# Loading x tile 0 through two queues, a later logarithm of the variances, and a new order of the leading TensorE work

## The chip, the cores and the metric

One Trainium2 chip, of which the kernel uses 1 core. The metric is the device time of one execution in microseconds (us), lower is better. The core has five engines that run at once: TensorE (PE, matrix multiply; its weight loads are shown apart as PEld), VectorE (DVE), ScalarE (ACT), GpSimd (POOL) and SyncE (SP, which here only issues transfers). ACT and POOL can issue transfers too. An engine takes its own instructions in order and waits for other engines on semaphores.

## The reference

Two branches over the same 2048 tokens of width 512 are mixed by a gate per token. Branch A is attention in a window of 8 keys at distance 2, with 32 heads of width 16. Branch B is a layer norm, followed by an MLP over the token axis.

```python
qkv = (x @ wqkv).reshape(B, S, 3, H, Dh)            # S 2048, D 512, H 32, Dh 16
idx = pos[:, None] - off[None, :]                   # off = 0, 2, ..., 14
logits = einsum("bhsd,bhswd->bhsw", q, kg) * scale  # masked where idx < 0
o = einsum("bhsw,bhswd->bhsd", softmax(logits), vg)
a = o.reshape(B, S, D) @ wo

h = (x2 - mean(x2)) / sqrt(var(x2) + 1e-5)          # over D, per token
u = gelu(einsum("bsd,sf->bdf", h, w1) + b1)         # S 2048, F 1792
y = einsum("bdf,fs->bds", u, w2) + b2
b = y.transpose(0, 2, 1)

g = sigmoid((x * gate_w).sum(-1, keepdims=True))
out = g * a + (1 - g) * b
```

The kernel takes the same x for both branches, and all tensors are bf16.

## The kernel before

Tokens come in 16 tiles of 128 rows. The work on TensorE has a fixed order, since each piece that is added through the helper `PE` (L570) is ordered behind the piece before it. On the other engines a list scheduler (`_Sched`, L75) sets the order from assumed durations and priorities, and the waits follow from which resource each operation reads and writes (`add`, L92). An `after` argument orders an operation behind the start of another one, without a semaphore.

TensorE goes through these stages.

- The head: six matmuls of ones (`f_warm`, L564), transposes of the tiles 0 to 3 of x (`tx`, L579), transposes of the biases b1 and b2 (`f_tb`, L594 and L595), a broadcast of the gate vector (L634), and the "leads" (L651 and L610). A lead t multiplies a strip of w1 (`lw`) with the normalized tile t (`lx`) into the banks 0 to 3. Lead 0 is done in two column halves.
- The projections of q, k and v (L716), whose input is x transposed. Their banks are 4 to 7, in a ring.
- The first MLP matmul (`f_ph2`, L601), with two sums of logits between (`f_sum`, L807).
- The second MLP matmul (`f_ph3`, L941) with the output projection (`f_wo`, L950), tile by tile, and the stores.

In the head, each of the first four tiles goes through a chain on two engines. On DVE there are `stat` (L615) and `aggr` (L619), which give mean and variance. On ACT, `rstd` (L622 and L623, both recorded under L469) takes a logarithm and an exponential, which need the table that ACT loads first (L1032). Then DVE normalizes the tile (`apply` L626, or L643 for the two halves of tile 0), and the lead may start. ACT copies transposed tiles out of PSUM (`ext`, L591), and the gate broadcast out of bank 6 (`evgw`, L659). Bank 6 also receives the transposes of tile 2, and bank 7 both those of tile 3 and the biases.

The tiles 4 to 15 are normalized later, all at once: DVE takes the statistics (L779) and combines them (L782 to L788), ACT takes the logarithm (`ln_log`, L789) and the exponential (`ln_rstd`, L790), DVE makes `ln_nmr` (L791). The tiles are then normalized in place by ACT (L795) for the last `LNACT` = 11 tiles, each ordered behind one copy of a projection out of PSUM (`ev2`, L748), and by DVE (L798) for the others, here tile 4 only. DVE also makes 16 gate sums (`z`, L760), which read the tiles of x before they are normalized, and the whole of the attention (L466).

Loads are issued on the queue of SP in the order of the program (`load`, L491, whose `order` argument chains them). Three small ones are on ACT's queue: b1, b2 and the gate vector. The very first load on SP's queue is tile 0 of x:

```python
def ld_x(t0, n):
    load("x%d" % t0, X[:, t0:t0 + n, :], xv[:, t0:t0 + n, :], n * 128 * D * 2, ["x%d" % t for t in range(t0, t0 + n)])

ld_x(0, 1)
ld_x(1, 1)
```

Of the kernel before, what the change touches and what calls it, by code (L numbers as in the profile page):

```python
# [9 lines left out]
AF = mybir.ActivationFunctionType  # L10
# [3 lines left out]
D = 512  # L14
# [14 lines left out]
NLEAD = 4  # L29
AVD = (1, 3, 5, 6)  # L30
GL = 4
NOUT = 8
LNACT = 11


class _Op:
# [281 lines left out]
def bass_gated_mix__sliding_local_dilated__mixer_token_mlp__prompt_kernel(nc, A_x, A_wqkv, A_wo, B_x, B_w1, B_b1, B_w2, B_b2, gate_w, out, dbg=None):  # L318
    with contextlib.ExitStack() as es:
# [39 lines left out]
        A = sch.add  # L359

        x2d = A_x[0]
# [6 lines left out]
        X = view("X", BF16, [(D, NST), (1, D)])  # L368
# [7 lines left out]
        def w2view(name, extra=0):  # L376
            return view(name, BF16, [(256, NFT), (1, 256)], extra=extra)

        XTALL = ["xt0_%d" % t for t in range(4)] + ["xt1", "xt2", "xt3"]
        W2S = [w2view(*W1SLOT[2]), w2view(*W1SLOT[3]), w2view(*W1SLOT[4]), w2view("P2"), w2view(*W1SLOT[0]), w2view(*W1SLOT[1]),  # L380
               w2view("X"), w2view("X", NFT * 256)]
        W2ALIAS = [["w1s2"], ["w1s3"], ["w1s4"], ["p2"], ["w1s0"], ["w1s1"],
                   ["x%d" % t for t in range(7)], ["x%d" % t for t in range(7, 14)]]
        XTUSE = ["w1s3", "w1s4"]
        PR = [["p0", "p0b"], ["p1", "p1b"], ["p2", "p2h"], ["log0", "log1", "att0", "att1", "lw0", "lw1", "lw2", "lw3", "gwr"]]
        LW = view("LOG", BF16, [(128 * GL, NLEAD), (1, 128 * GL)])
# [42 lines left out]
        ST6 = small(6 * NST, [(6, NST), (1, 6)])  # L429
# [8 lines left out]
        VV = small(NST)  # L438
# [6 lines left out]
        Z = small(NST)  # L445
# [6 lines left out]
        def col(v_, i):  # L452
            return bass.AP(v_.tensor, v_.offset + i, [list(v_.ap[0]), [1, 1]])
# [7 lines left out]
        def psub(ap_, p0, np_, offs, dims):  # L461
            pst = ap_.ap[0][0]
            return bass.AP(ap_.tensor, ap_.offset + p0 * pst + offs, [[pst, np_]] + [list(d) for d in dims])
# [4 lines left out]
        def act(o_, i_, f_, **kw):  # L468
            return lambda e: e.activation(out=o_, in_=i_, func=f_, **kw)  # L469
# [21 lines left out]
        def load(name, dst, src, nbytes, writes, transpose=False, queue="sp", issue=0.5, order=True, deps=(), reads=()):  # L491
            ds = sch.dsem(name)

            def fn(e):
                if transpose:
                    return e.dma_start_transpose(dst, src)
                return e.dma_start(dst, src)
            op = sch.dma(queue, fn, nbytes, ds, issue=issue, reads=reads, writes=writes, deps=deps,
                         after=([last_ld[0]] if order and last_ld[0] is not None else []), name=name)
            if order:  # L500
                last_ld[0] = op
            return op

        def ld_x(t0, n):
            load("x%d" % t0, X[:, t0:t0 + n, :], xv[:, t0:t0 + n, :], n * 128 * D * 2, ["x%d" % t for t in range(t0, t0 + n)])
# [11 lines left out]
        def ld_strip(t, n):  # L517
            load("s%d" % t, LW[:, t:t + n, :], w1v[:, t:t + n, 0:128 * GL], n * 32768 * GL, ["lw%d" % t_ for t_ in range(t, t + n)])

        ld_x(0, 1)  # L520
        ld_x(1, 1)
        ld_strip(0, 1)
        ld_x(2, 1)
# [46 lines left out]
        def PE(fn, dur, reads, writes, name, prio=0):  # L570
            op = A("pe", fn, dur, reads=reads, writes=writes, after=([chain[0]] if chain[0] is not None else []), name=name, prio=prio)
            chain[0] = op
            return op

        def f_tx(t):
            def fn(e):
                ins = None
                for dt in range(4):
                    ins = e.transpose(out=psb(4 + t)[:, dt * 128:dt * 128 + 128], in_=X[:, t, dt * 128:(dt + 1) * 128], identity=IDENT)  # L579
                return ins  # L580
            return fn

        def tx(t):
            PE(f_tx(t), 0.4, ["x%d" % t, "ident"], ["b%d" % (4 + t)], "tx%d" % t)

        def ext(t, eng, after):
            src = sub(psb(4 + t), 0, [(128, 4), (1, 128)])
# [24 lines left out]
            return fn  # L612

        def stat(t, after):
            return A("dve", (lambda t_: lambda e: e.bn_stats(out=ST6[:, t_, :], in_=X[:, t_, :]))(t), (0.69 if t == 0 else 0.58), reads=["x%d" % t], writes=["st%d" % t],  # L615
              after=after, name="st%d" % t, prio=-40)

        def aggr(t, after=()):
            return A("dve", (lambda t_: lambda e: e.bn_aggr(out=AG[:, t_, :], in_=ST6[:, t_, :]))(t), 0.17, reads=["st%d" % t], writes=["ag%d" % t], after=after, name="ag%d" % t, prio=-40)  # L619
# [5 lines left out]
        def apply(t, after):  # L625
            return A("dve", (lambda t_: lambda e: e.tensor_scalar(out=LX[:, t_, :], in0=X[:, t_, :], scalar1=AG[:, t_, 0:1], scalar2=col(RSTD, t_),  # L626
                                                                  op0=ALU.subtract, op1=ALU.mult))(t), 0.41, reads=["rstd%d" % t, "st%d" % t, "x%d" % t],
                     writes=["lx%d" % t], after=after, name="ln%d" % t, prio=-40)
# [1 line left out]
        PE(f_warm(6, 0), 2.6, [], ["b0"], "warm0")  # L630
        tx(0)
        tx(1)
        PE(f_tb, 0.2, ["b1r", "b2r", "ident"], ["b7"], "t_b12")
        PE(lambda e: e.matmul(ps[:, 6, :], lhsT=psub(WONE, 0, 1, 0, [(0, 128)]), rhs=GW1, start=True, stop=True), 0.4, ["gwr"], ["b6"], "gwbc")  # L634
        def lead(t):
            PE(f_lead(t), 0.87, ["lx%d" % t, "lw%d" % t], ["b%d" % ft for ft in range(GL)], "lead%d" % t)
# [5 lines left out]
        for q_ in range(2):  # L642
            l0 = A("dve", (lambda c_: lambda e: e.tensor_scalar(out=LX[:, 0, c_:c_ + 256], in0=X[:, 0, c_:c_ + 256], scalar1=AG[:, 0, 0:1],  # L643
                                                                scalar2=col(RSTD, 0), op0=ALU.subtract, op1=ALU.mult))(256 * q_), 0.22,
                   reads=["rstd0", "x0"], writes=["lx0%s" % "ab"[q_]], name="ln0%s" % "ab"[q_], prio=-40)
        e0 = ext(0, "act", [r0])
        def f_lead0(c0):
            def fn(e):
# [9 lines left out]
        r1 = rstd(1)  # L658
        ew = A("act", act(GWB, ps[:, 6, :], AF.Copy), 0.6, reads=["b6"], writes=["gwb"], after=[r1], name="evgw", prio=-50)  # L659
        tx(3)  # L660
        tx(2)
        s2 = stat(2, [ag])
        l1 = apply(1, [s2])
        ag = aggr(2, [l1])
        r2 = rstd(2)
        s3 = stat(3, [ag])
# [4 lines left out]
        e2 = ext(2, "act", [e1])  # L671
        e3 = ext(3, "dve", [l2])
        l3 = apply(3, [e3])
        for t in range(1, NLEAD):
            lead(t)
        e3 = l3
        A("dve", lambda e: e.tensor_copy(out=B1C, in_=psb(7)[:, 512:512 + NFT]), 0.15, reads=["b7"], writes=["b1c"], after=[e3], name="b1c", prio=-20)
        A("dve", lambda e: e.tensor_copy(out=B2C, in_=psb(7)[:, 544:544 + NST]), 0.15, reads=["b7"], writes=["b2c"], after=[e3], name="b2c", prio=-20)
# [57 lines left out]
        for dl in range(4):  # L736
# [3 lines left out]
          reads=["k%d_1" % dl for dl in range(4)], writes=["khalo"], name="khalo")  # L740
# [10 lines left out]
        ev2 = [[]]  # L751
# [6 lines left out]

        for t in range(NST):
            A("dve", (lambda t_: lambda e: e.tensor_tensor_reduce(out=JUNK[:, t_ % 4, :], in0=X[:, t_, :], in1=GWB, scale=1.0, scalar=0.0, op0=ALU.mult, op1=ALU.add,  # L760
                                                                  accum_out=col(Z, t_)))(t), 0.61, reads=["x%d" % t, "gwb", "s4"], writes=["z%d" % t, "jk%d" % (t % 4)], after=[e3],
              name="z%d" % t, prio=-4)
        A("pool", lambda e: e.memset(ZN, 0.0), 0.15, writes=["zn"], name="zn0")
        A("dve", lambda e: e.tensor_scalar(out=ZN[:, 0:NST], in0=Z, scalar1=ZMAX, scalar2=-1.0, op0=ALU.min, op1=ALU.mult), 0.12,
          reads=["z%d" % t for t in range(NST)], writes=["zn"], name="zneg", prio=-30)
# [20 lines left out]
        A("dve", lambda e: e.tensor_scalar(out=MS, in0=MS, scalar1=0.5, scalar2=None, op0=ALU.mult), 0.12, writes=["ms"], name="ln_mean", prio=-20)  # L786
        A("dve", lambda e: e.scalar_tensor_tensor(out=VV, in0=MD, scalar=128.0, in1=VV, op0=ALU.mult, op1=ALU.add), 0.12,
          reads=["md"], writes=["vv"], name="ln_var", prio=-20)  # L788
        A("act", act(VV, VV, AF.Ln, bias=1e-5, scale=1.0 / 512), 0.25, writes=["vv"], name="ln_log", prio=-20)  # L789
        A("act", act(RSTD2, VV, AF.Exp, scale=-0.5), 0.25, reads=["vv"], writes=["rstd"], name="ln_rstd", prio=-20)  # L790
        A("dve", lambda e: e.scalar_tensor_tensor(out=NMR, in0=MS, scalar=-1.0, in1=RSTD2, op0=ALU.mult, op1=ALU.mult), 0.12,  # L791
          reads=["ms", "rstd"], writes=["nmr"], name="ln_nmr", prio=-20)
# [290 lines left out]
```

## Time and profile before

| | us |
|---|---|
| median of 3 runs | 163.98 |
| lowest and highest of them | 163.47, 164.33 |
| the profiled execution | 163.24 |
| its span in the profile | 162.0 |
| of the span: TensorE busy | 159.0 |
| VectorE busy | 150.3 |
| ScalarE busy | 79.2 |
| GpSimd busy | 26.7 |
| head of TensorE, until the first projection matmul starts | 8.97 |

The profile describes one execution, from its first recorded instruction to its last. That span is 1.2 us shorter than the time of the same execution, and the time of the same execution is 0.7 us below the median of the three runs. A busy TensorE isn't TensorE at its peak, since matmuls overlap and their ends are modelled. How far apart matmuls start says more: in the projections 192 of them take 41.44 us, 0.216 us each.

### The profile page before, as it was taken

How to read it: one execution, taken by the hardware profiler on the slowest of the kernel's cores; microseconds unless marked ns; L12 is line 12 of the kernel's file. 1: busy time of each engine (PE TensorE's matmuls, PEld its weight loads, DVE VectorE, ACT ScalarE, POOL GpSimd, SP SyncE). 2: the span in 40 equal slices, each digit the busy share in tenths (PEclk: the TensorE clock that was granted, in tenths of full speed). 3: DMA queues.
4: the chain of work that ended last, by engine and by line, in shares of the span. 5: the costliest groups of instructions: out<-in, count | busy, mean ns of one | idle time of the engine just before them, and what ended most of it. 6: DMA issues, size and time to landing. Idle time of an engine off the chain costs nothing.

```text
span 162.0 us, 2018 instructions
## 1 busy us (share of the span) xinstructions
PE 159.0 (98%) x783; PEld 76.5 (47%) x783; DVE 150.3 (93%) x142; ACT 79.2 (49%) x105; POOL 26.7 (17%) x62
## 2 busy tenths in 40 slices
PE   7999999999999999999999999999999999999994
PEld 3555555555554344444444344444444444444652
DVE  2969999999999999999899999999999999999933
ACT  3727765799999472999211346320111111111153
POOL 3000011000000020200891030008770003020000
DMA  4999999999923999998499999999999815949404
GB/s 136 273 230 273 192 302 279 256 213 213 329 58 85 302 290 257 235 271 161 123 319 366 328 295 262 248 312 290 318 199 223 181 43 112 184 111 195 117 32 162
DMA packets 45288, 35.54 MB, mean 219 GB/s; under 512 B 8030, under 2 KB 42079, under 8 KB 45279
## 3 DMA queue, kind: packets, MB, share of 16 engines
q1 hardware_dynamic: 41376, 22.74, 53.0%
q0 software_dynamic: 3696, 12.59, 36.0%
q8 instruction: 6, 0.10, 0.3%
q10 hardware_dynamic: 206, 0.08, 0.2%
q14 instruction: 4, 0.02, 0.0%
HBM read 19.15 MB, written 2.11 MB: 131 GB/s over the span
## 4 chain that ended last, share of the span: by engine, by line
PE 98%; DVE 0%; issue 0%
PE ps L941 30%; PE ps L601 28%; PE ps L716 26%; PE ps L950 9%; PE ps L564 2%; PE ps L610 2%; PE ps L807 1%; PE ps L579 1%; PE ps L651 1%; DVE arena L959 0%; PE ps L634 0%; PE ps L594 0%; PE ps L595 0%
## 5 line engine op out<-in xcount | busy, mean ns | idle before, releaser
L466 DVE TENSOR_TENSOR arena<-arena 128x4096 bf16<-128x4096 bf16 (+8 forms) x71 | 125.8, 1806 | 1.7 <-DMA arena<-arena 0.5
L941 PE MATMUL ps<-arena 128*128 128x512 bf16 (+2 forms) x238 | 50.2, 366 | 0.0
L469 ACT ACTIVATE arena<-ps,arena 128x512 bf16<-128x512 f32 (+1 forms) x29 | 20.9, 728 | 56.5 <-PE ps L950 40.0
L601 PE MATMUL ps<-arena 128*128 128x512 bf16 x208 | 45.4, 379 | 0.0
L716 PE MATMUL ps<-arena 128*128 128x512 bf16 x192 | 41.6, 379 | 0.0
L469 ACT ACTIVATE arena<-ps 128x512 bf16<-128x512 f32 (+3 forms) x38 | 31.6, 843 | 11.0 <-PE ps L716 8.5
L941 PEld LDWEIGHTS ps<-arena 128*128 128x128 bf16 x238 | 23.3, 98 | 25.4
L601 PEld LDWEIGHTS ps<-arena 128*128 128x128 bf16 x208 | 20.2, 98 | 24.9 <-issue 0.8
L716 PEld LDWEIGHTS ps<-arena 128*128 128x128 bf16 x192 | 21.7, 113 | 19.8 <-ACT arena L469 0.2
L469 ACT ACTIVATE arena<-arena 128x512 bf16<-128x512 bf16 (+6 forms) x29 | 16.9, 581 | 11.1 <-DVE arena L466 9.0
L884 POOL DMA_DIRECT2D arena<-arena x32 | 17.1, 664 | 23.9 <-DVE arena L466 14.7
L950 PE MATMUL ps<-arena 128*128 128x512 bf16 (+2 forms) x68 | 15.6, 366 | 0.0
L835 POOL DMA_DIRECT2D arena<-arena x3 | 3.8, 1270 | 62.2 <-DVE arena L466 62.2
L1032 ACT ACT_TABLE_LOAD x9 | 11.5, 1283 | 2.3 <-issue 2.2
L760 DVE CUSTOM_DVE_ANT_0 arena<-arena 128x512 bf16<-128x512 bf16 x16 | 10.2, 686 | 0.0
L950 PEld LDWEIGHTS ps<-arena 128*128 128x128 bf16 x68 | 6.7, 98 | 7.2
L905 POOL DMA_DIRECT2D arena<-arena x4 | 4.9, 1226 | 30.6 <-DVE arena L466 30.6
L779 DVE BATCH_NORM_STATS2 arena<-arena 128x6 f32<-128x512 bf16 x12 | 7.4, 680 | 1.4 <-DMA arena<-in_A_x_dram 1.4
L615 DVE BATCH_NORM_STATS2 arena<-arena 128x6 f32<-128x512 bf16 x4 | 2.7, 670 | 3.0 <-DMA arena<-in_A_x_dram 3.0
L959 DVE TENSOR_SCALAR arena<-ps,arena 128x512 bf16<-128x512 f32 (+1 forms) x2 | 1.3, 660 | 3.8 <-PE ps L950 3.8
L564 PE MATMUL ps<-const-bfloat16-1.0 128*128 128x512 bf16 x6 | 2.7, 623 | 0.8 <-PEq L1068 0.8
L610 PE MATMUL ps<-arena 128*128 128x512 bf16 x12 | 2.8, 380 | 0.0
(41 smaller groups left out, 19.7 us busy)
## 6 DMA issues: line engine op xcount, KB each, us to landing
arena<-in_B_w_dram SPq DMA_DIRECT2D x8, 896.0 KB, 13.2
arena<-arena POOLq DMA_DIRECT2D x6, 1024.0 KB, 9.9
arena<-in_B_w_dram SPq DMA_DIRECT2D x5, 1024.0 KB, 9.1
arena<-arena POOLq DMA_DIRECT2D x32, 128.0 KB, 7.2
arena<-arena POOLq DMA_DIRECT2D x1, 2048.0 KB, 17.7
out_dram<-arena SPq DMA_DIRECT2D x15, 128.0 KB, 2.0
arena<-in_B_w_dram SPq DMA_DIRECT2D x2, 768.0 KB, 13.7
arena<-in_A_wqkv_dram SPq DMA_DIRECT2D x2, 512.0 KB, 5.3
```

What stands on the lines that cost most here:

```text
L466: return lambda e: e.tensor_tensor(out=o_, in0=a_, in1=b_, op=op_)
L469: return lambda e: e.activation(out=o_, in_=i_, func=f_, **kw)
L564: ins = e.matmul(ps[:, bank, :], lhsT=WONE, rhs=WROW, start=True, stop=True)
L601: ins = e.matmul(ps[:, bank, :], lhsT=W1S[W1AT[ft // 2]][:, st, 128 * (ft % 2):128 * (ft % 2) + 128], rhs=(LX if st < NLEAD else X)[:, st, :],
L610: ins = e.matmul(ps[:, ft, :], lhsT=LW[:, t, 128 * ft:128 * ft + 128], rhs=LX[:, t, :], start=(t == 0), stop=False)
L716: ins = e.matmul(ps[:, bank, :], lhsT=sub(WQKV, dt * 3 * D + tn * D + dl, [(4, 128)]), rhs=XT[:, dt, sb * 512:(sb + 1) * 512], start=(dt = ...
L760: A("dve", (lambda t_: lambda e: e.tensor_tensor_reduce(out=JUNK[:, t_ % 4, :], in0=X[:, t_, :], in1=GWB, scale=1.0, scalar=0.0, op0=ALU.m ...
L779: A("dve", (lambda t_: lambda e: e.bn_stats(out=ST6[:, t_, :], in_=X[:, t_, :]))(t), 0.6, reads=["x%d" % t], writes=["st%d" % t], after=[e ...
L884: prev = sch.dma("pool", (lambda d_, s_: lambda e: e.dma_start(d_, s_))(dst, src), 131072, ds, issue=1.0, reads=["att%d" % h], writes=["av ...
L941: ins = e.matmul(ps[:, bank, 0:c1 - c0], lhsT=W2S[i // 2][:, ft, 128 * (i % 2):128 * (i % 2) + 128], rhs=UT[:, ft, c0:c1], start=(ft == 0) ...
L950: ins = e.matmul(ps[:, bank, 0:c1 - c0], lhsT=OT[:, i // 2, dl, 128 * (i % 2):128 * (i % 2) + 128], rhs=WO[:, dl, c0:c1], start=False, sto ...
L1032: e.preload_act_table_set(want)
```

## The change

Four things are changed.

- Tile 0 of x is loaded as two transfers of 64 rows: rows 0 to 63 on SP's queue, rows 64 to 127 on ACT's queue. Everything that reads tile 0 waits for both.
- On TensorE, the transposes of the biases (`f_tb`) move from before the gate broadcast to behind the transposes of tile 3. The transposes of tile 2 move from before lead 1 to behind it.
- `ln_log` is ordered behind the fifth copy of a pair of projections (`ev2[0][4]`).
- `LNACT` goes from 11 to 9, so that ACT normalizes the tiles 7 to 15, and DVE the tiles 4 to 6.

```diff
-LNACT = 11
+LNACT = 9
...
+        def xr(t):
+            return ["x0a", "x0b"] if t == 0 else ["x%d" % t]
...
-        ld_x(0, 1)
+        for q_ in range(2):
+            load("x0%s" % "ab"[q_], psub(X, 64 * q_, 64, 0, [(1, D)]), x2d[64 * q_:64 * q_ + 64, :], 64 * D * 2, ["x0%s" % "ab"[q_]],
+                 queue=("sp", "act")[q_], order=q_ == 0)
         ld_x(1, 1)
...
-            PE(f_tx(t), 0.4, ["x%d" % t, "ident"], ["b%d" % (4 + t)], "tx%d" % t)
+            PE(f_tx(t), 0.4, xr(t) + ["ident"], ["b%d" % (4 + t)], "tx%d" % t)
...
         tx(0)
         tx(1)
-        PE(f_tb, 0.2, ["b1r", "b2r", "ident"], ["b7"], "t_b12")
         PE(lambda e: e.matmul(ps[:, 6, :], lhsT=psub(WONE, 0, 1, 0, [(0, 128)]), rhs=GW1, start=True, stop=True), 0.4, ["gwr"], ["b6"], "gwbc")
...
         tx(3)
-        tx(2)
+        PE(f_tb, 0.2, ["b1r", "b2r", "ident"], ["b7"], "t_b12")
         s2 = stat(2, [ag])
         l1 = apply(1, [s2])
+        lead(1)
+        tx(2)
...
-        for t in range(1, NLEAD):
-            lead(t)
+        lead(2)
+        lead(3)
...
-        A("act", act(VV, VV, AF.Ln, bias=1e-5, scale=1.0 / 512), 0.25, writes=["vv"], name="ln_log", prio=-20)
+        A("act", act(VV, VV, AF.Ln, bias=1e-5, scale=1.0 / 512), 0.25, writes=["vv"], after=[ev2[0][4]], name="ln_log", prio=-20)
```

The scheduler sets the order on DVE and ACT anew. In the order that it builds, ACT's queue holds the second half of tile 0 first, then the gate vector, b1 and b2, and then the table load. On ACT `ln_log` and `ln_rstd` stand behind five copies of projection pairs where they stood behind three. On DVE, `ln_nmr` comes behind six gate sums where it came behind one. The three normalizations of DVE stand behind the last gate sum, and all four products of the attention that stood around them (L466) follow. On TensorE the first sum of logits (L807) stands four matmuls later in the first MLP matmul. The order of DVE and ACT in the head is as before, and so is that of SP's and POOL's queues, apart from the halved load.

More of the change, by code (lines that the diff above doesn't have):

```diff
@@ L382, in bass_gated_mix__sliding_local_dilated__mixer_token_mlp__prompt_kernel @@
         W2ALIAS = [["w1s2"], ["w1s3"], ["w1s4"], ["p2"], ["w1s0"], ["w1s1"],
-                   ["x%d" % t for t in range(7)], ["x%d" % t for t in range(7, 14)]]
+                   [r_ for t in range(7) for r_ in xr(t)], ["x%d" % t for t in range(7, 14)]]
         XTUSE = ["w1s3", "w1s4"]
@@ L614, in stat @@
         def stat(t, after):
-            return A("dve", (lambda t_: lambda e: e.bn_stats(out=ST6[:, t_, :], in_=X[:, t_, :]))(t), (0.69 if t == 0 else 0.58), reads=["x%d" % t], writes=["st%d" % t],
+            return A("dve", (lambda t_: lambda e: e.bn_stats(out=ST6[:, t_, :], in_=X[:, t_, :]))(t), (0.69 if t == 0 else 0.58), reads=xr(t), writes=["st%d" % t],
               after=after, name="st%d" % t, prio=-40)
@@ L644, in bass_gated_mix__sliding_local_dilated__mixer_token_mlp__prompt_kernel @@
                                                                 scalar2=col(RSTD, 0), op0=ALU.subtract, op1=ALU.mult))(256 * q_), 0.22,
-                   reads=["rstd0", "x0"], writes=["lx0%s" % "ab"[q_]], name="ln0%s" % "ab"[q_], prio=-40)
+                   reads=["rstd0"] + xr(0), writes=["lx0%s" % "ab"[q_]], name="ln0%s" % "ab"[q_], prio=-40)
         e0 = ext(0, "act", [r0])
@@ L760, in bass_gated_mix__sliding_local_dilated__mixer_token_mlp__prompt_kernel @@
             A("dve", (lambda t_: lambda e: e.tensor_tensor_reduce(out=JUNK[:, t_ % 4, :], in0=X[:, t_, :], in1=GWB, scale=1.0, scalar=0.0, op0=ALU.mult, op1=ALU.add,
-                                                                  accum_out=col(Z, t_)))(t), 0.61, reads=["x%d" % t, "gwb", "s4"], writes=["z%d" % t, "jk%d" % (t % 4)], after=[e3],
+                                                                  accum_out=col(Z, t_)))(t), 0.61, reads=xr(t) + ["gwb", "s4"], writes=["z%d" % t, "jk%d" % (t % 4)], after=[e3],
               name="z%d" % t, prio=-4)
```

## The prediction

> **What bounds the kernel now.** I read the engine shares first, then the chain that ended last.
>
> ```profile
> PE 159.0 (98%) x783; PEld 76.5 (47%) x783; DVE 150.3 (93%) x142; ACT 79.2 (49%) x105; POOL 26.7 (17%) x62
> ...
> PE 98%; DVE 0%; issue 0%
> ```
>
> ```profile
> 0.84 2.72 PE ps L564 x6
> 3.56 0.85 PE ps L579 x8
> ...
> 6.49 2.65 PE ps L610 x12
> 9.13 41.44 PE ps L716 x192
> 50.57 5.18 PE ps L601 x24
> ```
>
> Columns of the second: start, length, what. The chain is TensorE from end to end. From the first projection (it starts at 8.97) 192 matmuls take 41.44 us, 0.216 each, and the later stages keep that pace. In the starts of the single matmuls no stop shows between 8.97 and 159.6 but some 0.1 us of switching before and behind each of the two L807 groups. So time can be won in the head alone, and lost where a stop is made. Third, the timeline of the head (start, length, engine, what, idle time before it and who ended it):
>
> ```profile
> 0.81 0.86 SPq L497 DMA_DIRECT2D arena<-in_A_x_dram  x2
> 0.82 1.00 ACTq L497 DMA_DIRECT2D arena<-in_B_b_dram  x2
> 1.85 0.29 ACTq L497 DMA_DIRECT2D arena<-in_gate_w_dram  x1
> 2.17 1.28 ACT L1032 ACT_TABLE_LOAD   x1 [2.17 <-issue]
> 2.97 0.69 DVE L615 BATCH_NORM_STATS2 arena<-arena 128x6 f32<-128x512 bf16 x1 [2.97 <-DMA arena<-in_A_x_dram]
> 3.91 0.44 ACT L469 ACTIVATE arena<-arena 128x1 f32<-128x1 f32 x2 [0.45 <-DVE arena L619]
> 4.83 0.77 PEld L651 LDWEIGHTS ps<-arena 128*128 128x128 bf16 x8 [0.33 <-DVE arena L643]
> 6.08 0.23 PEld L579 LDWEIGHTS ps<-arena 128*128 128x128 bf16 x4 [0.16 <-ACT arena L469]
> 7.23 1.41 PEld L610 LDWEIGHTS ps<-arena 128*128 128x128 bf16 x8 [0.38 <-DVE arena L626]
> ```
>
> Tile 0 lands, DVE starts at 2.97, ACT's logarithm at 3.91, lead 0 at 4.83. Later TensorE waits for the gate copy (6.08) and for tile 2 (7.23). ACT's table load ends at 3.45, only 0.45 us before its first use. And the matmul durations of the head (ns min/median/max, then first and last start):
>
> ```profile
> L610 PE MATMUL ps<-arena x12: 379/379/389, 6.3 to 8.8; 128*128 128x512 bf16 x12
> ...
> L564 PE MATMUL ps<-const-bfloat16-1.0 x6: 585/631/631, 0.8 to 2.9; 128*128 128x512 bf16 x6
> ```
>
> One and the same shape takes 631 ns at first (0.427 us from start to start) and 379 later (0.216), although the granted clock is shown as 1.00 in both stretches. L634, at 4.42, has 479 ns, in between; so the fast rate came at about 4.6.
>
> **Tile 0 in two halves.** Now it costs one SP issue of 0.39 us and reaches DVE 2.16 us after 0.81. By the traffic of the first 4 us (150 to 390 GB/s once loads run), its 128 KB take about 0.5 us of those. If the halves run fully side by side, tile 0 lands up to 0.25 earlier; if they share the same transfer engines, not at all. The late end is ACT's issue: its first one took 0.65 us (b1, 14 rows) against SP's 0.39, and a half behind such an issue lands 0.26 late. So -0.25 to +0.26; nearest is SP's own row, so about -0.1.
>
> The Trainium skill, page "DMA: Bandwidth & Descriptors", section "Rules for kernel authors", speaks against this edit: on two transfers to disjoint partition halves it says "Don't bother — they serialize", since both spread over the same 16 engines. By the rule this term is 0, by the row's better end -0.25, and the total below is the same for both.
>
> For the gain is cut off on ACT's queue. The table load stands behind every issue there: now b1 0.65, b2 0.33, gate 0.29, then 2.17 to 3.45. The half adds one issue, 0.33 (b2's row) to 0.43 (SP's 128-row loads, 0.39 to 0.43), or 0.65 if both it and b1 are as dear as b1; with 0.03 between issues that is +0.36 to +0.68. The table is ready at 3.81 to 4.13. The logarithm starts 0.03 later: 3.84 to 4.16, against 3.91. I take +0.42: 3.90, no change. Queued behind it are both ACT steps of tile 0, the DVE halves of L643, and lead 0. On SP the issue is shortened at most to b2's 0.33, which brings the other loads 0.06 earlier; they are covered (x1 has landed at 3.41 and is read at 3.80).
>
> **The TensorE order in the head.** No work goes. Before the gate broadcast, `f_tb` with its switch costs 0.21 (the tile 1 transposes end at 4.21, the broadcast starts at 4.42). Without it there is still a switch from 128 rows to 1: I give back 0.07, the time between `f_tb`'s own start at 4.35 and 4.42; ends 0 and 0.21. The broadcast runs from 4.35 and ends about 0.04 earlier, as it then runs longer at the slow rate. Lead 0, bound by DVE's half (done at 4.73) and by TensorE (free at about 4.8), starts at 4.79 to 4.83.
>
> From 4.83 on: lead 0 takes 0.88 (to 5.71), tile 3 0.23 (5.94). Then `f_tb`, 0.21 with its switch (0.05 if the switch is free, 0.35 if there are two): 6.15. Lead 1, whose tile DVE finishes at 6.00, starts at 6.15, where it now starts at 6.32, because tile 2's transposes and the wait of 0.15 stood before it. It ends at 7.02; tile 2's transposes take 0.23: 7.25. Lead 2 starts there; DVE's tile 2 (7.23) is ready. Now it starts at 7.24. So moving `f_tb` fills two waits with the time it left behind: +0.01, or -0.03 with the earlier broadcast. Queued behind tile 2's transposes is ACT's copy, which now starts at 7.74 behind tile 1's copy; transposes that end at 7.25 don't hold it, and the first projection has its copy at 8.33. Bounds for the head: all stops behind 4.21 vanish, 0.13 + 0.11 + 0.15 + 0.05 = -0.44; or the table at its late end, 4.16 - 3.91 = +0.25, with 0.15 more for a dear `f_tb`: +0.40. Taken: 0.0.
>
> **The logarithm later, nine tiles on ACT.**
>
> ```profile
> 29.92 0.46 ACT L469 ACTIVATE arena<-arena 128x16 f32<-128x16 f32 x2 [0.73 <-DVE arena L787]
> ```
>
> ```profile
> 31.35 0.83 PEld L716 LDWEIGHTS ps<-arena 128*128 128x128 bf16 x5 [0.25 <-ACT arena L469]
> ```
>
> The two small ACT operations push the fourth pair's copy from 29.89 to 30.29, and one weight load waits 0.25 for it; the matmuls show no gap. Moved behind the fifth copy (ends 32.55) they fit into ACT's idle time until the next, 33.34. Worth 0 on the path. DVE then needs the result behind six gate sums, 30.11 + 6 x 0.61 = 33.8; it is there at 33.0. ACT's last normalization still stands before the last copy (49.80 to 50.60), and it is needed at 51.43, four matmuls into L601.
>
> DVE gets two tiles more, at 0.33 each (L798 starts at 35.82, the next at 36.14): +0.65. Cover: DVE's last sum before the first L807 group ends at 54.88, and that group starts at 55.69. It now stands four matmuls later, 56.55; DVE is done at 55.53, 1.0 to spare. At the second group, 89.17 against 91.30; at the last `wo` that waits for tile 6, 155.23 against 156.86. Each holds +0.65. Without the cover the whole 0.65 would be paid once.
>
> **The sum.** 0.0 + 0 + 0 on the span of 162.0. The profiled execution (163.24) was 0.7 below the median; I take the change onto the runs, whose median is 163.98 and whose mean with the profiled one is 163.76: 163.9.
>
> The spread of 1.1 us between executions may be the time at which the fast rate comes: the Trainium skill, page "TensorE: Matmul & The Clock Gate", section "Part 1: The HAM clock gate", has a window of about 3.4 us that runs free of the kernel. No row of one execution can show that.
>
> **The rivals.** Forecast, no change: 163.9, own range 163.4 to 164.4; 0.72. For it is a TensorE that never stops behind 8.97.
>
> *The head closes up.* Tile 0 is early, ACT's issues are cheap, the switches vanish: -0.44, 163.5. For: four stops are in the trace. Against: the table load, 0.45 from binding. 0.12.
>
> *The table load takes the place of the tile.* Logarithm at 4.16, dear `f_tb`: +0.40, 164.3. For: b1's issue of 0.65; against: the next two cost half. 0.08.
>
> *The fast rate comes later (slower).* If the altered stops before lead 0 make TensorE stay slow, lead 0's eight matmuls start 0.213 apart instead of 0.109: +0.87, and with tile 3 and lead 1 as well +1.96, less 0.2 of waits that vanish. It decides from a fast rate later than about 5.7. Price between 0.7 and 1.8, at 1.2: 165.1. For: the rate changed just before lead 0. Against: stops of 0.1 us were there before. 0.08.
>
> That the halves gain nothing since they serialize is inside the forecast.
>
> **The numbers.** About 0.5% (0.82 us) is what a measurement of this kernel tells from no change. Faster means below 163.16: 0.06 of the forecast by spread and 0.4 of the closed head, 0.04 + 0.05 = 0.09. Slower means above 164.80: 0.04, 0.2 of the table case 0.02, 0.8 of the slow rate 0.06: 0.12. Rest 0.79. The range goes from below the closed head, 163.2, to above the table case, 164.7, leaving out the slow rate.
>
> **What would show it.** Right: table load ending near 3.9, logarithm at 3.9 with no idle before it, the projections from about 8.97, a pace of 0.216 to the end, DVE's last sum done about 1.0 us ahead of the first L807 group. Wrong: projections from before 8.6 or after 9.3, head matmuls at 0.427 later than 5.7, or a stop of TensorE before either sum of logits.

## The result, and the profile after

| | before | after |
|---|---|---|
| median, us | 163.76 | 164.54 |
| lowest and highest | 163.16, 164.41 | 163.78, 166.08 |
| runs | 22 | 22 |
| ratio with its 95% interval | | 1.0055 [1.0031, 1.0078] |
| profiled execution | 163.24 | 165.51 |
| its span | 162.0 | 164.3 |

The changed kernel is slower. Its median says little, since no run lies near it: eleven runs take 163.78 to 163.83 and eleven take 165.24 to 166.08. The kernel before has one group. In all the comparisons of this study it ran 121 times, and none took more than 164.66. The profiled execution of the changed kernel is one of the second group.

The engine shares of its page, and the chain that ended last:

```profile
PE 161.1 (98%) x783; PEld 77.3 (47%) x783; DVE 151.3 (92%) x144; ACT 77.8 (47%) x103; POOL 26.7 (16%) x62
...
PE 96%; ACTq 1%; ACT 1%; DVE 1%; issue 0%
```

TensorE issues the same 783 matmuls and is busy 2.1 us longer. And the chain no longer is TensorE from end to end: some 4% of it lies elsewhere. The chain in order of time (start, length, what) shows where:

```profile
0.81 0.54 ACTq L500
...
1.39 0.78 ACTq L500
...
2.19 0.40 ACTq L500
...
2.62 0.38 ACTq L500
...
3.03 1.28 ACT L1038
...
4.33 0.21 ACT arena L472
...
4.80 0.36 DVE arena L647
```

The first 5 us of the chain are now ACT's four issues, its table load, the logarithm of tile 0 and its normalization. Then comes lead 0. The timeline of the head (start, length, engine, what, idle time before it and who ended it):

```profile
0.80 1.45 SPq L500 DMA_DIRECT2D arena<-in_A_x_dram  x2
3.20 0.69 DVE L620 BATCH_NORM_STATS2 arena<-arena 128x6 f32<-128x512 bf16 x1 [3.20 <-DMA arena<-in_A_x_dram]
3.92 0.34 PEld L584 LDWEIGHTS ps<-arena 128*128 128x128 bf16 x4 [0.21 <-DMA arena<-in_A_x_dram]
4.33 0.44 ACT L472 ACTIVATE arena<-arena 128x1 f32<-128x1 f32 x2
4.47 0.60 PE L638 MATMUL ps<-arena,const-bfloat16-1.0 1*128 1x512 bf16 x1
5.20 1.89 PE L655 MATMUL ps<-arena 128*128 128x256 bf16 x8
7.60 1.86 PE L615 MATMUL ps<-arena 128*128 128x512 bf16 x4
9.28 0.40 PE L584 MATMUL ps<-arena 128*128 128x128 bf16 x4
9.51 1.89 PE L615 MATMUL ps<-arena 128*128 128x512 bf16 x8
11.24 2.97 PE L722 MATMUL ps<-arena 128*128 128x512 bf16 x13
```

Three things are to be seen. Tile 0 is later (3.20 against 2.97), and tile 1, whose landing used to be covered, now stops TensorE until 3.92. The logarithm starts at 4.33 with no idle time before it, 0.02 behind the table load: the table has become the later of the two. And the fast matmul rate is missing: lead 0's eight matmuls of 256 columns take 1.89 from 5.20, so they start 0.213 apart, and the four of lead 1, of 512 columns, take 1.86, 0.427 apart; the eight of leads 2 and 3 take 1.89 from 9.51, 0.216 apart. Here the fast rate came at about 9.3; before, it came at about 4.6. The granted clock doesn't tell of it. In the view by stretches (stretch, length, busy time of each engine with its count, then the granted clock, the DMA share and GB/s) it is 1.00 at the slow rate too:

```profile
4.00:8.00 4.00, 3.87 (x21) 2.19 (x22) 3.74 (x12) 3.15 (x12) 0.00 (x0) 1.00 0.89 246
11.24:52.70 41.46, 41.46 (x194) 21.73 (x193) 38.62 (x58) 31.27 (x43) 1.42 (x1) 1.00 0.99 217
```

How long does TensorE stand still ahead of lead 0? Counted from start to start, an estimate is 0.15 before tile 1's transposes (the four of tile 0 start 0.107 apart from 3.35 on, and tile 1's first one starts at 3.93) and 0.30 before lead 0 (the gate broadcast, L638, starts at 4.47 and has 512 columns, 0.427 at the slow rate).

From the first projection on nothing has changed. The projections start at 11.24 instead of 8.97, 2.27 later, and the profiled execution is 2.27 longer. Time less the start of the first projection is 154.27 in both. So the whole loss is made in the head.

The changed kernel was profiled once more (e8 below), and that execution, of 163.87, is one of the first group:

```profile
3.17 1.28 ACT L1038 ACT_TABLE_LOAD   x1 [3.17 <-issue]
3.50 0.71 PE L584 MATMUL ps<-arena 128*128 128x128 bf16 x8
5.34 1.05 PE L655 MATMUL ps<-arena 128*128 128x256 bf16 x8 [0.81 <-DVE arena L647]
6.79 1.02 PE L615 MATMUL ps<-arena 128*128 128x512 bf16 x4
9.60 3.62 PE L722 MATMUL ps<-arena 128*128 128x512 bf16 x15
```

The same program, the same late table, lead 0 even later (5.34). But the rate changes while the transposes run, at about 3.8, ahead of the stop of 0.81. Lead 0's eight matmuls take 1.05 instead of 1.89, and lead 1's four 1.02 instead of 1.86. From lead 0 to the first projection it is 4.26 us here and 6.04 in the other group: 1.78 is what the late rate costs.

### The profile page after: what moved, and what is told of

Its sections match the earlier page's. It is cut to its first block, busy times and chain, and to the rows that moved or that the text cites. A ratio compares the mean times of both kernels' runs of the same rounds, so it can differ in the third digit from the quotient of the medians.

```text
span 164.3 us, 2019 instructions
## 1 busy us (share of the span) xinstructions
PE 161.1 (98%) x783; PEld 77.3 (47%) x783; DVE 151.3 (92%) x144; ACT 77.8 (47%) x103; POOL 26.7 (16%) x62
## 4 chain that ended last, share of the span: by engine, by line
PE 96%; ACTq 1%; ACT 1%; DVE 1%; issue 0%
PE ps L947 29%; PE ps L606 27%; PE ps L722 25%; PE ps L956 8%; PE ps L615 2%; ACTq L500 1%; PE ps L813 1%; PE ps L655 1%; ACT L1038 1%; PE ps L584 0%; DVE arena L965 0%; ACT arena L472 0%; DVE arena L647 0%; PE ps L599 0%; PE ps L600 0%
## 5 line engine op out<-in xcount | busy, mean ns | idle before, releaser
L469 DVE TENSOR_TENSOR arena<-arena 128x4096 bf16<-128x4096 bf16 (+6 forms) x71 | 125.7, 1806 | 1.9 <-ACT arena L472 0.4
L472 ACT ACTIVATE arena<-arena 128x512 bf16<-128x512 bf16 (+6 forms) x27 | 15.2, 565 | 9.3 <-DVE arena L469 8.4
```

Of the source, the lines that this page charges most:

```text
L469: return lambda e: e.tensor_tensor(out=o_, in0=a_, in1=b_, op=op_)
```

## The experiments

Two questions were put. Which part of the change costs the time? And what makes the second group: theory A1, that a stop of TensorE ahead of lead 0 makes it miss the moment at which the fast rate is granted; A2, that the head is merely later; or something later than the head? In each comparison the kernel before ran on the same chip; the ratio is to its runs. The comparisons themselves ran on four chips: one each for e1 to e4, e5 to e8, e9 to e12, and e13 to e16.

### e1 to e4: the parts of the change

e1 has the two halves of tile 0 alone, e2 the TensorE order alone, e3 the later logarithm with nine tiles alone, and e4 is the change without the two halves.

```diff
# e1: before, with
-        ld_x(0, 1)
+        for q_ in range(2):
+            load("x0%s" % "ab"[q_], psub(X, 64 * q_, 64, 0, [(1, D)]), ..., queue=("sp", "act")[q_], order=q_ == 0)
# e2: before, with f_tb behind tx(3), and lead(1) before tx(2)
# e3: before, with LNACT = 9 and ln_log after=[ev2[0][4]]
# e4: after, with ld_x(0, 1)
```

> The kernel before with only tile 0 of x loaded in two halves, on SP's and ACT's queue. Theory A (the split is the cause: ACT's table load and tile 0 come late, TensorE stops some 0.3 us before lead 0, and in part of the executions the slow matmul rate then holds until about 9): lead 0 at 5.1 to 5.3 instead of 4.83, median 164.2 to 165.2, times in two groups. Theory B (the new order on TensorE is the cause, since it takes the bias transposes out of the stretch before lead 0): no change, 163.5 to 164.0. Theory C (the later work of DVE and ACT): no change.

> The kernel before with only the order on TensorE changed: bias transposes behind those of tile 3, tile 2's transposes behind lead 1. Theory A: 163.4 to 163.9, no group above 164.6, projections from 8.9 to 9.0 in an execution with an early fast rate. Theory B: a median of 164.2 or more with a second group above 165.

> The kernel before with only the logarithm of the variances ordered behind the fifth copy and nine tiles normalized on ACT. Theories A and B: no change, 163.5 to 164.0, the matmul pace from 9 to the end as before. Theory C: slower by 0.5 or more, with a stop of TensorE at a sum of logits.

> The changed kernel with tile 0 of x loaded at once on SP's queue again; order on TensorE and the later logarithm stay changed. Theory A: the loss is gone, 163.4 to 163.9, no second group. Theory B: as the changed kernel, median 164.3 to 165. Theory C: slower than before by 0.5 or more.

| 12 runs each | median | lowest, highest | over 165 | ratio |
|---|---|---|---|---|
| e1 halves | 164.25 | 163.87, 165.94 | 5 | 1.0049 [1.0019, 1.0079] |
| e2 order | 163.75 | 163.31, 164.51 | 0 | 0.9995 [0.9978, 1.0012] |
| e3 logarithm, nine tiles | 163.63 | 163.24, 164.05 | 0 | 0.9990 [0.9973, 1.0007] |
| e4 all but the halves | 163.73 | 163.31, 164.25 | 0 | 0.9993 [0.9979, 1.0006] |

The halves alone make the whole loss, the second group included; everything else together makes nothing that can be measured. The timeline of e1, whose profiled execution (165.46) is of its second group, has both ends of it:

```profile
0.80 1.46 SPq L500 DMA_DIRECT2D arena<-in_A_x_dram  x2
0.81 0.56 ACTq L500 DMA_DIRECT2D arena<-in_A_x_dram  x1
1.40 1.20 ACTq L500 DMA_DIRECT2D arena<-in_B_b_dram  x2
2.96 1.28 ACT L1037 ACT_TABLE_LOAD   x1 [2.96 <-issue]
4.25 0.44 ACT L472 ACTIVATE arena<-arena 128x1 f32<-128x1 f32 x2
4.38 0.61 PE L584 MATMUL ps<-arena 128*128 128x128 bf16 x4 [0.39 <-DMA arena<-in_A_x_dram]
```

On ACT's queue the half's issue moves the table to 2.96 and the logarithm to 4.25. On SP's queue the first half and tile 1 take 1.46 to issue where two whole tiles took 0.86, and tile 1 reaches TensorE at 4.38 only; from start to start, TensorE stands still for about 0.6 there. Lead 0 starts at 5.50, later than expected.

e2 and e4 also have ACT's queue in its new order, the gate vector ahead of b1 and b2, with all loads whole. This is e2:

```profile
0.81 0.52 ACTq L497 DMA_DIRECT2D arena<-in_gate_w_dram  x1
1.35 0.78 ACTq L497 DMA_DIRECT2D arena<-in_B_b_dram  x2
2.17 1.28 ACT L1033 ACT_TABLE_LOAD   x1 [2.17 <-issue]
```

The table load starts when it did before, at 2.17, so the new order costs nothing. And with all loads whole, the first issue on ACT's queue is the long one: the gate vector takes 0.52 here and 0.29 as the last one in before, and b1 takes 0.65 as the first in before and 0.35 as the second here.

### e5 and e8: matmuls in the stops, and the change again

e5 is the change with two matmuls of ones, of 256 columns each, whose result nobody reads: one behind tile 0's transposes, one behind the gate broadcast. e8 is the change as it is.

```diff
+        PE(f_fill(1), 0.0, [], ["b1"], "fill0")      # behind tx(0)
+        PE(f_fill(2), 0.0, [], ["b2"], "fill1")      # behind the gate broadcast
```

> The changed kernel with two matmuls of ones, 256 columns each, put into TensorE's stops: one behind the transposes of tile 0, one behind the gate broadcast. Nothing else moves, and the loads are as late as before. Theory A1 (the slow rate lasts because TensorE stops just before lead 0; the fast rate wants a stretch of unbroken work): the group above 165 is gone or rare, all executions from 163.7 to 164.6, median 163.8 to 164.1, although work was added. Theory A2 (late transfers themselves cost the time, the clock only follows): two groups as in the changed kernel, median 164.2 to 165.2.

> The changed kernel once more, for a profile. If the execution falls at 163.8: fast rate before or at lead 0, lead 0 at 5.2 as in the first profile, projections from 9.4 to 9.7 (the loads' part of the loss, 0.4 to 0.7). If it falls above 165: as the first profile.

e5: median 164.07 (163.79 to 165.95, 12 runs), ratio 1.0021 [0.9996, 1.0045]. Eleven of twelve runs are below 164.5, and one is at 165.95. With more work on TensorE, put into the stops, fewer executions fall into the second group than in the change: one of twelve instead of eleven of 22. That speaks for A1, though a single run remained.

### e6: a late table with whole loads

Before, with one ScalarE copy of 128x512 that nobody reads ahead of the first logarithm.

```diff
+        A("act", act(JUNK[:, 0, :], ..., AF.Copy), 0.0, reads=["ones"], writes=["jk0"], ..., name="late", prio=-100)
```

> The kernel before, with one copy of 128x512 on ACT behind its table load, so that ACT's first logarithm starts at 4.1 to 4.3 instead of 3.91. The loads stay as they were, and TensorE stops 0.2 to 0.4 before lead 0. A1: two groups, 163.6 to 164.5 and above 165, with the fast rate at about 9 in the second. A2: one group, later by at most the 0.2 to 0.4 of the delay, 163.7 to 164.6, none above 165.

Median 163.97 (163.54 to 164.45, 12 runs), ratio 1.0002 [0.9982, 1.0021]. It decides nothing: the copy took 0.63, from 3.48 to 4.11, so that the logarithm moved by 0.1 only and TensorE stopped for 0.09. Its profile (163.98) showed something else. From the projections' start on it takes 0.65 more than before's (154.92 against 154.27), and the stop stands at the old place of `ln_log`:

```profile
30.69 0.46 ACT L469 ACTIVATE arena<-arena 128x16 f32<-128x16 f32 x2 [1.42 <-DVE arena L788]
31.06 1.92 ACT L469 ACTIVATE arena<-ps 128x1024 bf16<-128x1024 f32 x2
32.37 1.46 PE L717 MATMUL ps<-arena 128*128 128x512 bf16 x6 [0.70 <-ACT arena L469]
```

The two small operations wait 1.42 for DVE, and the copy behind them, with it TensorE, 0.70. DVE is late because a tile of x is: it starts its statistics of the later tiles at 12.77, after 2.05 of waiting for the load, where before started them at 12.00, while the projections start only 0.08 later than in before. On SP's queue the transposing load ahead of it took 6.02 to issue instead of 5.28; why is open, as no load was touched. With the logarithm in its new place no profile here has this stop.

### e7: both halves on SP's queue

```diff
-                 queue=("sp", "act")[q_], order=q_ == 0)
+                 queue="sp")
```

> The changed kernel with both halves of tile 0 on SP's queue. If it is the second queue (both queues issue at once and hold each other up, and ACT's table load stands behind the half): issues of 0.33 to 0.43 on SP, table load from 2.1 to 2.2, tile 0 read at 2.9 to 3.2, median 163.5 to 164.0, no group above 165. If two halves are dear on any queue: issues above 0.5, tile 0 read at 3.2 or later, median above 164.2.

Median 165.78 (164.11 to 166.20, 7 runs), ratio 1.0109 [1.0071, 1.0147], five of the seven above 165. The halves' issues took 0.57 and 0.58, that of tile 1 behind them 0.58 too, and DVE got tile 0 at 3.77. ACT's table was as early as before (2.15 to 3.43). So the second queue isn't what makes the halves dear. Two of them in a row make tile 0 late by themselves, by 0.8. And the second group is there with the table as early as before, so late tiles alone are enough for it.

### e9, e13, e14: the stop alone, filled, and longer

These leave all the loads whole. e9 is e3 with two ScalarE copies ahead of the first logarithm, so that lead 0 comes late for a reason that has nothing to do with transfers. e13 has two matmuls of ones in the stop that e9 makes. e14 has four copies. e15 and e16 are e9's kernel again.

```diff
# e9, on e3 (e14: range(4))
+        for q_ in range(2):
+            A("act", act(JUNK[:, q_, :], ..., AF.Copy), 0.0, reads=["ones"], writes=["jk%d" % q_], ..., name="late%d" % q_, prio=-100)
# e13, on e9, behind the gate broadcast
+        PE(f_fill(2, 512), 0.0, [], ["b2"], "fill0")
+        PE(f_fill(1), 0.0, [], ["b1"], "fill1")
```

> The kernel before with its later logarithm and nine tiles, no split and the old TensorE order, and two ScalarE copies (128x512, 0.63 each as the one copy took) put ahead of the first logarithm. No load is touched. The logarithm starts at about 4.65 instead of 3.91 and lead 0 at about 5.5 instead of 4.83, with one stop of TensorE of some 0.7 us before it. Theory A1 (a stop ahead of lead 0 is enough to let the fast matmul rate be missed once): two groups, some runs in 5 to 9 of 12 above 165.0, median 164.3 to 165.2. Theory A2 (it takes stops at the transposes too, that is late loads): one group, 163.9 to 164.9, each run later by the 0.4 to 0.7 that lead 0 is late, none above 165.1.

> The kernel of e9 with two matmuls of ones (512 and 256 columns) behind the gate broadcast, in the stop before lead 0. Lead 0 waits for the same late logarithm, at about 5.4. If the stop of TensorE makes the second group: none of 12 runs above 165.0, all between 163.7 and 164.7. If the lateness of lead 0 makes it: 3 to 7 of 12 above 165.0 as in e9.

> The kernel of e9 with four ScalarE copies ahead of the first logarithm instead of two: lead 0 at 6.2 to 6.7, the stop before it 0.8 us longer. If a stop that covers the moment of the rate change makes it be missed, a longer stop covers more: 6 to 10 of 12 runs in the second group, against 5 of 12, and both groups later by 0.6 to 1.2, the first at 164.4 to 165.0, the second above 165.8. If the share does not depend on the stop's length, 4 to 6 of 12.

> The kernel of e9 again, for a profile. In the first group (163.8): matmuls at 0.216 per 512 columns from about 3.5. In the second (above 165): the slow pace, 0.427, up to 9.0 to 9.5, lead 0 at about 5.4 with eight matmuls 0.213 apart, the first projection matmul at 11.0 to 11.6.

> The same as the run before it: matmuls at the fast pace from about 3.5 and 163.8, or at the slow pace up to 9.0 to 9.5 and above 165.

| | median | lowest, highest | over 165 | ratio |
|---|---|---|---|---|
| e9, two copies | 163.85 | 163.83, 165.96 | 5 of 12 | 1.0046 [1.0012, 1.0079] |
| e13, the stop filled | 163.84 | 163.81, 164.25 | 0 of 12 | 1.0019 [1.0006, 1.0031] |
| e14, four copies | 166.29 | 164.85, 167.43 | 5 of 6 | 1.0142 [1.0109, 1.0175] |

e9 has the second group with all loads whole. e13 waits as long for the same logarithm and has none. e14's first group has one run, 164.85, and the others are at 166.01 and above. (The ratio of e14 leaves out the execution of 167.43, for which nothing here gives a reason.) A2 falls: lead 0 is about as late in e9 (5.38) as in e13 (5.55), and only the one in which TensorE stands still has the second group. e9 and e13 ran on different chips, but on e13's chip e14 has the second group, and on e9's chip e10 (below), filled, has none. Whether a longer stop makes the second group more frequent is not settled: five of six against five of twelve differ by chance in about one case of seven. In the timelines, first e9:

```profile
3.35 0.67 PE L579 MATMUL ps<-arena 128*128 128x128 bf16 x8
5.38 1.05 PE L653 MATMUL ps<-arena 128*128 128x256 bf16 x8 [0.98 <-DVE arena L645]
```

This execution, of 163.84, is of the first group. The rate changed among the transposes, at about 3.5, and the stop of 0.98 came behind that. Then e13:

```profile
4.42 0.58 PE L637 MATMUL ps<-arena,const-bfloat16-1.0 1*128 1x512 bf16 x1
4.94 0.82 PE L584 MATMUL ps<-const-bfloat16-1.0 128*128 128x512 bf16 x2
5.55 1.25 PE L658 MATMUL ps<-arena 128*128 128x256 bf16 x8
```

The ones fill the time to 5.55, and within lead 0 (1.25, between 1.05 and 1.89) the rate changes, at about 6.0. Then e14, an execution of 166.01:

```profile
4.42 0.58 PE L634 MATMUL ps<-arena,const-bfloat16-1.0 1*128 1x512 bf16 x1
6.42 1.89 PE L653 MATMUL ps<-arena 128*128 128x256 bf16 x8 [1.42 <-DVE arena L645]
8.95 2.92 PE L610 MATMUL ps<-arena 128*128 128x512 bf16 x12
11.70 1.03 PE L718 MATMUL ps<-arena 128*128 128x512 bf16 x4
```

A stop of 1.42, all eight matmuls of lead 0 at the slow rate, the fast one from about 9.3. The three profiles of e9's kernel (e9, e15 and e16, 163.84 each) fell into its first group, and in all three the rate had changed ahead of the stop: at about 3.5, 4.5 and 3.8. For e15 the gate broadcast shows it: it took 0.40, against 0.58 at the slow rate in e14 and 0.37 at the fast one in e9. That its second group is the same late rate is inferred from e14 and from its price (165.41 to 165.96, 1.6 to 2.1 more), and was not seen in a profile.

### e10: the stops of the change filled

e5 with a third and more matmuls of ones: 256 columns behind each of the first two transposed tiles, 512 behind the broadcast.

```diff
+        PE(f_fill(1), 0.0, [], ["b1"], "fill0")         # behind tx(0)
+        PE(f_fill(3), 0.0, [], ["b3"], "fill1")         # behind tx(1)
+        PE(f_fill(2, 512), 0.0, [], ["b2"], "fill2")    # behind the gate broadcast
```

> The changed kernel with three matmuls of ones whose result nobody reads: 256 columns behind the transposes of tile 0, 256 behind those of tile 1, 512 behind the gate broadcast. The loads are as late as in the changed kernel, but TensorE stops less. Clock theory: no run above 165.0, all between 163.7 and 164.7, median about 164.0 (0.1 to 0.3 above the kernel before: the lateness of tile 0 alone). If the second group comes from the loads themselves or from something later than the head, 4 to 7 of 12 runs stay above 165.0.

Median 163.80 (163.79 to 164.52, 12 runs), none above 165, ratio 1.0008 [0.9993, 1.0024]. The loads and the table are as late as in the change (3.39 for tile 0, 3.19 to 4.48 for the table), lead 0 starts at 5.37, and the second group is gone.

### e11 and e12: what makes an issue dear

e11 is the kernel before with tile 3 in two halves of 64 rows, tile 0 whole. e12 has tile 0 in two halves of 256 columns, all 128 rows each. Both are on SP's queue.

```diff
# e11
-        ld_x(3, 1)
+        for q_ in range(2):
+            load("x3%s" % "ab"[q_], psub(X, 64 * q_, 64, 3 * D, [(1, D)]), ...)
# e12
-        ld_x(0, 1)
+        for q_ in range(2):
+            load("x0%s" % "ab"[q_], X[:, 0, 256 * q_:256 * q_ + 256], xv[:, 0, 256 * q_:256 * q_ + 256], ...)
```

> The kernel before with tile 3, the fourth x tile on SP, loaded as two halves of 64 rows; tile 0 whole. If loads of 64 rows are dear to issue wherever they stand: 0.54 to 0.60 each against 0.39 to 0.43 for the whole tiles beside them, 0.7 us more on SP's queue. If only the first loads of a queue are dear: 0.39 to 0.43 each. Time 163.2 to 164.6 either way, as tile 3 has slack.

> The kernel before with tile 0 in two halves of 256 columns, all 128 rows each, both on SP. If the 64 rows make an issue dear: two issues of 0.39 to 0.43, x1 issued about 0.42 later than before, tile 0 at DVE at 3.0 to 3.4. If a second transfer of one tile is dear in any shape: 0.54 to 0.60 each, tile 0 at 3.7 as with two row halves on one queue. Time 163.8 to 166: one look doesn't decide it, the issues do.

One line of the head of each, e11 and then e12:

```profile
2.18 1.66 SPq L497 DMA_DIRECT2D arena<-in_A_x_dram  x3
```

```profile
0.81 1.34 SPq L497 DMA_DIRECT2D arena<-in_A_x_dram  x3
```

Both are three issues. In e12, two column halves and tile 1: 1.34, that is 0.39, 0.41 and 0.42 with the gaps. In e11, tile 2 and two row halves: 1.66, that is 0.43, 0.55 and 0.59, and the strip of w1 behind them took 0.585 before the next was at 0.43 again. So on SP's queue it is the 64 rows, not the second transfer and not the place in the queue, that makes an issue dear, and the next issue pays as well. On ACT's queue the half always stood first, where any issue takes longer (e2 above), so there the two causes can't be told apart. e11 took 164.63 in its single run, above what was expected: tile 3 has slack, but the loads behind it have not. TensorE stopped at 12.81 for the projection weights, and at 33.03 for 1.06 at the old place of the logarithm. e12 took 164.38 in its single run, with the same stop, 0.59, at 32.76.

## Why the prediction was wrong

The forecast, 163.9 with no change, held for half of the executions (163.8) and missed the other half, which is the rival "the fast rate comes later" at 0.08. The median, 164.54, falls in the empty space between the two; that it lies inside the stated range, 163.2 to 164.7, is luck. Luck is also that the first group comes so near the forecast: its projections start 0.6 later than was forecast (9.60 in e8), as the last table below shows.

*Tile 0 in two halves: the step that failed.* The prediction added one issue to ACT's queue, +0.42 and at most +0.68, and put its effect on the issue behind it at nothing. The half took 0.54; b1, no longer first, took 0.25 less than before (0.40 for 0.65), and b2 0.05 more. With the gap of 0.03 these come to 0.37, about what was taken. But the gate vector's issue, behind the half, took 0.78 instead of 0.29, and this 0.48 was in no term. The sum is +0.86: the table is ready at 4.31, and the logarithm starts at 4.33 where 3.90 was taken and 4.16 was the late end. Nothing in the trace of before had a load of 64 rows. And b1's 0.65 was read as the price of its 14 rows, where e2 shows it to be that of the first place.

On SP, the prediction took the half for cheaper and the loads behind it for covered. The half took 0.58 for the 0.39 of the whole tile, and tile 1 behind it 0.82 for 0.41. Tile 1 had landed at 3.41 and was read at 3.80, a cover of 0.39; the two dear issues ate it, and tile 1 landed at 3.88. For tile 0 itself -0.25 to +0.26 held in this profile (+0.23) but not in e8 (3.46, +0.49). The Trainium skill's rule in "DMA: Bandwidth & Descriptors", section "Rules for kernel authors", that such halves serialize and aren't worth it, was right in its advice; e7 shows a loss where the rule speaks only of no gain. Whether the halves serialize, no run here shows.

*The fast rate: the mechanism was named, its condition was misjudged.* It was to decide from a rate later than about 5.7, and was held unlikely because stops of 0.1 us had been harmless. But the stops did not stay at 0.1. The late table and the late tile 1 make stops of 0.15 and 0.30 us in the profile of after, 0.6 in e1's and 0.81 in e8's, and e9, e13 and e14 show that a stop ahead of lead 0 is enough. What failed is that a late table was priced only as a delay, +0.25, and not as a stop of TensorE that opens the other rival. The two were one chain. The size was good, with some luck: 1.96 less 0.2 were worked out, and 1.78 was measured between the two groups. By the starts in the traces the three pieces come to 0.83 for lead 0 (8 x 0.104), 0.20 for tile 3 (4 x 0.051) and 0.84 for lead 1 (4 x 0.211), 1.88 rather than 1.96.

*The TensorE order: right.* 0.0 was taken, and e2 measured 0.9995 [0.9978, 1.0012]. In the profile after, its small waits can't be compared step by step, since the rate differs there. In e4's they can: the same order, all loads whole, the fast rate from about 4.0.

```profile
6.17 1.04 PE L610 MATMUL ps<-arena 128*128 128x512 bf16 x4
...
7.28 1.90 PE L610 MATMUL ps<-arena 128*128 128x512 bf16 x8
...
9.02 2.75 PE L717 MATMUL ps<-arena 128*128 128x512 bf16 x11
```

Lead 1 starts at 6.17 where 6.15 was taken, lead 2 at 7.28 where 7.25 was, and the projections at 9.02, 0.05 later than in the profile of before.

*The logarithm later, nine tiles: right in its sum.* e3 measured 0.9990 [0.9973, 1.0007]. The timeline of after at this place shows it as predicted, TensorE without a stop across it:

```profile
27.64 8.58 PE L722 MATMUL ps<-arena 128*128 128x512 bf16 x39
...
33.89 1.02 ACT L472 ACTIVATE arena<-ps 128x1024 bf16<-128x1024 f32 x1 [0.70 <-PE ps L722]
34.81 0.46 ACT L472 ACTIVATE arena<-arena 128x16 f32<-128x16 f32 x2
```

DVE's cover for its two further tiles held: the first L807 group (L813 after) starts at 58.82, 47.58 behind the projections, the 47.58 that the prediction's 56.55 less 8.97 gives. That this edit guards against a late load of the later tiles, worth 0.65 in e6, was not in the prediction. A late head by itself does not make that stop: e1 and e2, with the logarithm in its old place and the projections at 11.18 and 9.71, don't have it.

*The spread of before* was put down to the moment of the fast rate. The runs bear that out from the other side. In before, e2 and e3 the rate was seen at 4.6, 6.3 and 5.7, and the projections started at 8.97, 9.71 and 9.16. In the three profiles of e9's kernel lead 0 waits for ScalarE until 5.38 wherever the rate changed before that (at about 3.5, 3.8 and 4.5), and all three took 163.84. That fits the changed kernel's first group, which is only 0.05 wide. But it is not the only candidate for the spread of before: the stop at the old place of the logarithm (0.70 in e6, 1.06 in e11, 0.59 in e12) would lengthen an execution as well. Before was profiled once, so how much each of the two gives is open.

| profiled execution | lead 0 | fast rate from about | first projection | time | time less projection |
|---|---|---|---|---|---|
| before | 4.83 | 4.6 | 8.97 | 163.24 | 154.27 |
| after | 5.20 | 9.3 | 11.24 | 165.51 | 154.27 |
| after again (e8) | 5.34 | 3.8 | 9.60 | 163.87 | 154.27 |
| e9 | 5.38 | 3.5 | 9.56 | 163.84 | 154.28 |
| e13, stop filled | 5.55 | 6.0 | 9.67 | 163.95 | 154.28 |
| e14, stop longer | 6.42 | 9.3 | 11.70 | 166.01 | 154.31 |

The table also gives the first group's own loss. Lead 0 is 0.4 to 0.5 later and the projections 0.6 later than in the profile of before. That is +0.6 against before's best runs, and next to nothing against its median, since before loses as much when its rate is late (e2's profile: projections at 9.71).

No version beat the kernel before: e3 and e4 have the lowest medians, and both intervals hold 1.

*What stays open.* The moment at which the rate is decided is in no view, so what share of the time TensorE has to be busy is not known. In the profiles of e8, e9, e15 and e16 the change had come before the stop began; in e14 it had not come ahead of a stop of 1.42, and the fast rate was there at 9.3 only. But not every stop at the change does harm: in e7's profile (164.37, first group) TensorE stood still for 0.45, from start to start, ahead of the first transpose at 3.81, and the rate changed within that stop. The Trainium skill, page "TensorE: Matmul & The Clock Gate", section "Part 1: The HAM clock gate", has a window of some 3.4 us that runs free of the kernel, and grants the fast rate behind a busy one. The runs agree as far as they go: the rates seen at 3.5 to 6.3 lie within one such window, and the late ones at 9.2 to 9.3 are, as an estimate, one window behind 5.9, where the filled e13 got its rate (6.0). It would also say why the groups differ from run to run. But a share of busy time in such a window does not sort the runs, again as an estimate: the one that would end with e9's change, at 3.5, holds 0.75 us ahead of the first matmul (0.84), and the rate was granted; the one that would end at 5.9 in the profile of after holds some 0.6 without a matmul (0.15, 0.30, and 0.14 ahead of the gate broadcast), and it was not. No run here shows the window itself.

## What to carry to other kernels

A transfer that is split costs issues on every queue that it touches, and here it slowed the issue behind it as well. Take the price of an issue from a row of the same shape and the same place in the queue, and if there is none, bound it by more than the nearest rows, and ask what each load and each table load behind it is covered by. And where the head of a kernel waits for a faster matmul rate, a stop of some tenths of a microsecond ahead of it can cost far more than its own length: here a delay of 0.4 us cost 1.8 more, in half of the executions. A median between two groups tells of neither, so look at the single runs first.

## What the runs showed of the hardware

- An issue of a load of 64 rows took 0.54 to 0.59 us on either queue (on ACT's always in the first place), against 0.39 to 0.43 on SP's for 128 rows of 512 (before) or of 256 columns (e12). The issue behind it was slowed as well: to 0.57 to 0.83 on SP's queue, for 128 rows, and to 0.69 to 0.92 on ACT's, for the gate vector or b1.
- The first issue on ACT's queue took longer than the same load in a later place: the gate vector 0.52 (e2) against 0.29 (before), b1 0.65 (before) against 0.35 (e2).
- The matmul rate changed by a factor of two (0.427 to 0.216 us for 512 columns) while the granted clock read 1.00 throughout the profile after.
- With a stop of TensorE ahead of lead 0 the fast rate came at about 9.3 in e14; with two matmuls in the stop whose result nobody reads (e13) it came at about 6.0.
